# Two attentions in one kernel: normalisation in place in PSUM, eight score slots for VectorE, other staging buffers, hinted branches, and an order planned anew with five more VectorE tiles

## The chip, the core and the metric

The kernel runs on one core of a Trainium2 chip. The metric is the device time of one execution in microseconds (us). Before the change it is 740.9 us, the median of three runs (740.27 to 741.24). TensorE is called PE here (PEld is its weight load), VectorE DVE, ScalarE ACT, GpSimd POOL and SyncE SP.

## What is computed

Two attention blocks over different inputs of the same size (S = 2048 tokens, D = 640, H = 32 heads of 20), their outputs side by side:

```
def _A_ref(x, wqkv, wo):                      # softmax attention
    qkv = (x @ wqkv).reshape(B, S, 3, H, Dh) -> q, k, v per head
    p = softmax(einsum("bhqd,bhkd->bhqk", q, k) * Dh ** -0.5)
    return einsum("bhqk,bhkd->bhqd", p, v) -> (B, S, D) @ wo

def _B_ref(x, wqkv, wo):                      # linear attention
    phi = lambda t: where(t > 0, t + 1, exp(t)) + 1e-6
    num = phi(q) @ (phi(k)^T v);  den = phi(q) . sum_s phi(k) + 1e-6
    return (num / den) -> (B, S, D) @ wo

return concatenate([a, b], axis=-1)
```

A has 32 heads x 2048 x 2048 scores, and each needs an exponential. That is the bulk of the work.

## The kernel before, in words

**Head groups and score tiles.** The 32 heads are taken four at a time, the 2048 queries 512 at a time: 8 x 4 = 32 *head groups*, numbered n = 0 to 31 (`self.od`). Each has 16 key tiles of 128, and a key tile has four score units (one head each) of 128 x 512. A score unit is one matmul `f_Qr,f_KT` in a quarter of PE's rows; several of them, on different rows, run side by side.

**Two ways to an exponential.** Most key tiles go to ACT: two units at a time lie in a pair of PSUM banks (a *score group*; pairs 0, 1 and 2, 3 take turns), and one activation (L1880) writes 2 x 512 exps into two of the 16 slots of `f_PT`. With 146 tiles on the other way there are (512 - 146) x 4 / 2 = 732 such exps. The other 146 tiles, chosen by the list `DN` (how many of the five key tiles in `DKT` each head group gives away), go to DVE: it converts the scaled scores to int16 (L1778), so that the bits read as a bf16 are a rough power of two; POOL adds a constant into a second buffer (`int64_add`, L1964), a DMA with accumulate (issued by POOL at L1962, 512 KB) adds that buffer back on the first one, and POOL adds another constant (L1956). The first sum is used with V, the second with a scaled copy `f_Vp`, as two more PV terms. The buffers are `f_Sr`: `NS` = 4 slots for the first sum and `NY` = 3 for the second.

**PV and normalisation.** Per head group all PV matmuls (`f_PT,f_V`, `f_Sr,f_V`, `f_Sr,f_Vp`) add up in one PSUM bank, number 4 (`PVB`); groups go strictly one after the other. V's first column is one, so the bank holds the denominators too. `norm` (L1967 to L1992) ends a group on DVE: a 32 x 32 block transpose of the bank into `f_T` in SBUF, fp32 (L1991), after which the bank is free for the next group (`freed`); a reciprocal of the denominators (L1982); the multiply into `f_T2` (L1984); the transpose back into `f_OTn` (L1988). SP then copies the heads' rows into `f_OTd` by small DMAs (L2017), from which the output projection reads.

**The rest of PE's work** is the projections of A (`f_xT,f_wq`, `f_xT,f_ar`, `f_ar,f_xT` for Q, K and V), the output projections (`f_wo,f_OTd`, `f_wo,f_OTn`, and `f_ar` with 128 or 512 columns for B), all of B, and *fillers*, matmuls of zeros (`f_zt`) that keep PE's utilisation up. These *auxiliary* works and the DVE score tiles share the banks 5, 6 and 7. A wide matmul here has 512 columns; most come in fours (`quad`) that fill the four column tiles of the array side by side.

**The order.** Nothing is scheduled on the chip: while the program is built, `_Fast.run` plays the five engines against a clock of its own. Each pick takes the engine that is free first (`self.free`); `est` says when the operands and buffers of an operation are there; `try_pe` chooses among score group, PV, DVE tile, auxiliary step and filler, `try_q` the runnable operation of lowest `prio` on the other engines. `emit` and `burst` then write the instruction into that engine's stream and book a cost. So the costs in the class (`CDMA`, `LDMA` for the accumulating DMA, `SW` for a change of the matmul kind, the latency in `push`) and the goals (`B0`, `B1`, `DOUBLE`, `LASTD`, the `P` priorities) decide the order, and on the chip each engine walks through its list and waits, in order, for semaphores.

**Output staging.** `evac` copies a bank of a finished output projection into one of five 512-wide parts of `f_st` (L1009 on DVE, L1008 on ACT) and queues an output DMA on SP (L1006), with priority -1 (first) if the step's own priority is at most 0, else 55. x's first 512 rows land in `f_st` too, before it is used for that (`start_loads`).

**The end.** A flag is made on the chip from the reciprocals (it says whether all denominators are in range). All engines load it into a register (L2311), and `nc.If(val > 0)` (L2312, shown as L202 in the profile) runs a general version, `_general`, if it is set; on these inputs all engines branch over it, and SP waits for the last output DMAs.

## Time and profile before

| | |
|---|---|
| median of 3 runs | 740.9 us (740.27 to 741.24) |
| the profiled execution | 740.83 us; 739.1 us of it from the first to the last instruction (the span) |
| mean granted PE clock | 0.987 of full speed |
| ACT | 699.4 us busy, 732 exps at L1880 |
| DVE | 617.2 us busy |
| POOL | 455.1 us busy |
| PE | 711.8 us busy (ends modelled) |

How to read the lines in the prediction. A timeline row is start, length, engine, line, operation, out<-in, shapes, count, and in square brackets the idle time ahead of it with what ended it. A waits row is who waited <- for whom: sum, times, longest, in us. A row of a single line or tile gives shortest, median and longest duration in ns, then the first and last start. Buffer numbers are left out: `f_T` stands for `f_T` and `f_T2`, `ps` for any PSUM bank. A row in the window table has, behind its window and length, busy time and count of PE, PEld, DVE, ACT and POOL, then the granted PE clock, the DMA engines' busy share and GB/s. Engine names that end in q are the sequencer's own instructions (branches, semaphores, DMA issues).

### The profile page before, as it was taken

The page shows a single profiled execution, that of the slowest core. Times are in us where ns is not written, and L with a number is a line of the kernel's source. Part 1 is how long each engine was busy: PE and PEld are TensorE (multiplying, and loading weights), DVE is VectorE, ACT ScalarE, POOL GpSimd, SP SyncE. Part 2 cuts the span into 40 slices and gives each one's busy share as a digit, 9 for nine tenths or more (in the row PEclk, how much of TensorE's full clock was granted, in tenths as well). Part 3 has the DMA queues.
Part 4 walks back from the last instruction along what each step waited for, and adds up shares of the span by engine and source line. Part 5 has one row for each costly group of instructions (what it writes and reads, how often), then busy time and mean ns, then how long its engine had stood idle before and what let it go on. Part 6 is the DMA issues. An engine that isn't in the chain of part 4 may idle for free.

```text
span 739.1 us, 24693 instructions
## 1 busy us (share of the span) xinstructions
PE 711.8 (96%) x10762; PEld 247.1 (33%) x10762; DVE 617.2 (84%) x1087; ACT 699.4 (95%) x778; POOL 455.1 (62%) x469
## 2 busy tenths in 40 slices
...
GB/s 197 191 164 107 134 124 151 123 149 186 171 176 155 151 145 136 129 126 98 128 112 150 129 186 137 157 159 136 104 178 146 169 158 68 143 106 81 153 156 68
DMA packets 68107, 104.12 MB, mean 141 GB/s; under 512 B 33707, under 2 KB 48747, under 8 KB 67995
## 3 DMA queue, kind: packets, MB, share of 16 engines
...
q14 instruction: 28, 0.22, 0.1%
...
## 4 chain that ended last, share of the span: by engine, by line
ACT 63%; PE 18%; DMA 8%; DVE 6%; POOL 3%; issue 1%; SPq 1%; ACTq 0%; DVEq 0%
ACT f_PT L1880 61%; PE ps L166 18%; DMA f_Sr<-f_Sr 6%; DVE f_Sr L1778 3%; ACT f_ar L1415 2%; POOL f_KT L1147 1%; DMA f_OTd<-f_OTn 1%; POOL f_Sr L1964 1%; DVE f_ar L1417 1%; DMA f_ar<-in_A_wqkv_dram 1%; SPq L2017 1%; DVE f_T L1984 1%; DVE f_T L1991 0%; DVE f_OTn L1988 0%; POOL f_V L1131 0%
## 5 line engine op out<-in xcount | busy, mean ns | idle before, releaser
L1880 ACT ACTIVATE f_PT<-ps 128x1024 bf16<-128x1024 f32 x732 | 684.6, 1112 | 24.5 <-PE ps L166 23.7
L1778 DVE TENSOR_SCALAR f_Sr<-ps 128x512 int16<-128x512 f32 x584 | 390.4, 683 | 71.0 <-PE ps L166 65.6
L166 PE MATMUL ps<-f_Qr,f_KT 32*128 32x512 bf16 x2048 | 300.2, 387 | 8.9 <-ACT f_PT L1880 3.4
L1964 POOL INT64_ADD f_Sr<-f_Sr x146 | 154.0, 1055 | 170.7 <-DVE f_Sr L1778 153.5
L1956 POOL INT64_ADD f_Sr<-f_Sr x146 | 167.7, 1151 | 63.9 <-DMA f_Sr<-f_Sr 61.5
L166 PEld LDWEIGHTS ps<-f_Qr,f_KT 32*128 32x128 bf16 x2048 | 76.4, 91 | 255.5 <-ACT f_PT L1880 218.8
L166 PE MATMUL ps<-f_ar 128*32 128x512 bf16 (+6 forms) x3024 | 146.5, 297 | 0.9 <-DVE f_Sr L1778 0.6
L1962 POOL DMA_DIRECT2D f_Sr<-f_Sr x146 | 127.7, 875 | 30.4 <-POOL f_Sr L1964 28.8
L166 PE MATMUL ps<-f_PT,f_V 128*21 128x512 bf16 x1464 | 141.1, 386 | 0.2 <-DVE f_T L1991 0.2
L166 PEld LDWEIGHTS ps<-f_ar 128*32 128x32 bf16 x3024 | 56.5, 95 | 57.3 <-issue 36.8
L166 PE MATMUL ps<-f_Sr,f_V 128*21 128x512 bf16 x584 | 58.3, 384 | 4.6 <-DMA f_Sr<-f_Sr 3.9
L166 PE MATMUL ps<-f_Sr,f_Vp 128*21 128x512 bf16 x584 | 58.8, 388 | 0.3 <-POOL f_Sr L1956 0.2
L166 PEld LDWEIGHTS ps<-f_PT,f_V 128*21 128x21 bf16 x1464 | 35.6, 90 | 49.6 <-issue 41.8
L166 PE MATMUL ps<-f_zt 128*32 128x256 bf16 (+2 forms) x184 | 36.6, 291 | 1.6 <-DVE f_warm L1089 1.1
L166 PE MATMUL ps<-f_ar,f_xT 128*32 128x160 bf16 x1280 | 35.7, 234 | 0.3 <-DMA f_ar<-in_A_wqkv_dram 0.3
L166 PE MATMUL ps<-f_wo,f_OTd 128*32 128x512 bf16 (+3 forms) x608 | 30.6, 302 | 2.4 <-DMA f_OTd<-f_OTn 2.4
L1991 DVE STREAM_TRANSPOSE f_T<-ps 128x512 f32<-128x512 f32 x32 | 22.7, 708 | 12.1 <-PE ps L166 12.0
L166 PE MATMUL ps<-f_xT,f_ar 128*32 128x512 bf16 x400 | 31.7, 383 | 0.0
L1009 DVE CAST f_st<-ps 128x512 bf16<-128x512 f32 x38 | 25.8, 684 | 6.5 <-PE ps L166 6.3
L1417 DVE TENSOR_SCALAR f_ar<-f_ar 128x512 bf16<-128x512 bf16 x40 | 24.2, 606 | 8.4 <-ACT f_ar L1415 7.7
L1984 DVE TENSOR_TENSOR f_T<-f_T,f_Rt 128x512 bf16<-128x512 f32 x32 | 27.8, 869 | 0.3
L166 PEld LDWEIGHTS ps<-f_ar,f_xT 128*32 128x32 bf16 x1280 | 22.9, 96 | 15.3 <-issue 11.8
...
## 6 DMA issues: line engine op xcount, KB each, us to landing
f_Sr<-f_Sr POOLq DMA_DIRECT2D x146, 512.0 KB, 5.1
out_dram<-f_st SPq DMA_DIRECT2D x40, 128.0 KB
...
```

The costliest lines, as they stand in the source:

```text
L166: lambda e: e.matmul(out, lhsT, rhs, start=start, stop=stop, tile_position=tp, skip_group_check=sgc),
L1009: (lambda e: e.tensor_copy(sl, ps[:, b, 0:w])), (("ps", b),), (("stage", s),),
L1147: self.push("pool", lambda e, g=g: e.tensor_copy(self.KT[:, g, :], self.kb16[:, 1:2].broadcast_to([128, self.S])), ("kb16",), tuple(("K", ...
L1415: self.push("act", lambda e: e.activation(r1, src, AF.Exp), (("ps", b),), (rk,), _c_act(n), prio=0, ok=ok, after=lambda: self.push("dve", ...
L1417: "dve", lambda e: e.tensor_scalar(r1, r1, 1.0, 1e-6, op0=ALU.min, op1=ALU.add), (rk,), (rk,),
L1778: post = lambda: self.push("dve", lambda e: e.tensor_scalar(self.Sr[:, s, i, :], self.ps[:, b, :], 0.0, 32639.0 - self.PH[-1], op0=ALU.max ...
L1880: return _Op("act", lambda e: e.activation(self.PT[:, s0:s0 + n, :], ps[:, b0:b0 + n, :], AF.Exp, scale=math.log(2.0) / 128.0, bias=self.l ...
L1956: put(lambda e: e.int64_add(vy, vy, up2), (), ry, self.C64, self.C64 + 150, fin)
L1962: put(lambda e: e.dma_start(flat(a).bitcast(BF16), flat(y).bitcast(BF16), accum_op=ALU.add), ry, ra, self.CDMA, self.LDMA, third).dma = True
L1964: put(lambda e: e.int64_add(vy, va, up), ra, ry, self.C64, self.C64 + 150, add, lambda: d < self.NY or self.dphase[d - self.NY] == 2)
L1984: "dve", lambda e: e.tensor_tensor(T2v, Tv, R.unsqueeze(2).broadcast_to([128, 16, 32]), op=ALU.mult),
L1991: self.push("dve", lambda e: e.transpose(self.T[:], ps[:, b, :]), (("ps", b),), ("T",), 630, prio=-1, after=freed, ok=lambda: n == 0 or (" ...
```

## The change

Eight edits in one:

1. **Normalisation in place.** The first transpose writes back into bank 4; reciprocal and multiply read the bank; only after the multiply is the bank free. `f_T` (fp32, SBUF) is gone. All three operations now have priority -1.
2. **Slots.** `NS` is 5, so that `f_Sr` has 8 slots for 7.
3. **VectorE tiles.** `DN` sums to 151 for 146.
4. **Planner's costs and goals.** `LDMA` 6500 for 6000; each accumulating DMA starts, in the plan, no sooner than 2900 ns after the one before (`dfree`), with 2000 ns more in the first 32 us; SP's operations land 3200 ns after their issue for 2000; `DOUBLE`, `B1`, `P1`, `P3`, `LASTD`, `SW` have other values.
5. **Staging.** `f_st` has 3 parts of 512 for 5; the last five tiles of A's output are staged in exp buffers (`f_PT`, slot p), without the ring; only these have SP priority -1, all others 55.
6. **x's first rows** land in slots 8 to 12 of `f_PT`.
7. **Zeros.** `f_zt` is 128 wide and is read twice by a broadcast of stride 0; the ring for `f_OTn` has a name (`RING` = 3, as before); small tiles share one.
8. **Branch.** `nc.If` is written out as a compare-and-branch on each engine with two blocks, and each branch has a hint whose place is at the normalisation of head group 30 of 0 to 31.

```
     NPT = 16
-    NS = 4
+    NS = 5
     NY = 3
     CDMA = 880.0
...
-    LDMA = 6000.0
+    LDMA = 6500.0
...
-    DOUBLE = 0.0
+    DOUBLE = -8.0
...
-    DN = (4, 3, 4, 5, 5, 4, 5, 5, 5, 4, 5, 5, 4, 4, 5, 4, 5, 5, 5, 5, 5, 4, 5, 5, 5, 5, 3, 5, 4, 4, 5, 5)
+    DN = (4, 5, 4, 4, 5, 5, 4, 5, 5, 4, 5, 5, 5, 4, 5, 4, 5, 5, 5, 4, 5, 5, 4, 5, 5, 5, 5, 5, 5, 5, 5, 5)
...
-    LASTD = 8
+    LASTD = 4
...
-    SW = 112.0
+    SW = 107.0
...
+        if op.dma and e == "pool":
+            s = max(t + 1450.0, self.dfree)
+            self.dfree = s + 2900.0
+            op.lat += s - t - 1450.0 + (2000.0 if t < 32000.0 else 0.0)
...
-        x = {"dve": 150, "act": 180, "pool": 150, "sp": 2000}[eng]
+        x = {"dve": 150, "act": 180, "pool": 150, "sp": 3200}[eng]
...
-    def evac(self, b, o, w, eng, prio, dst, done):
+    def evac(self, b, o, w, eng, prio, dst, done, pt=None):
         ps = self.ps
-        s = self.slot(o)
-        sl = self.stage[:].rearrange("p t n -> p (t n)")[:, 512 * s:512 * s + w]
-        end = prio <= 0
+        if pt is None:
+            s = self.slot(o)
+            sl, res = self.stage[:, s, 0:w], ("stage", s)
+        else:
+            sl, res = self.PT[:, pt, 0:w], ("PT", pt)
+        end = pt is not None
...
+        if n == self.NN - 2:
+            self.hints = {e: self.nc.engines[e].mark_branch_hint_location() for e in mybir.ALL_ENGINES}
...
-        Tv = self.T[:].rearrange("p (b c) -> p b c", c=32)
+        Tv = ps[:, b, :].rearrange("p (b c) -> p b c", c=32)
...
-        self.push("dve", lambda e: e.transpose(self.T[:], ps[:, b, :]), (("ps", b),), ("T",), 630, prio=-1,
-                  after=freed, ok=lambda: n == 0 or ("OTn", n - 1) in self.done)
+            self.push("dve", lambda e: e.transpose(self.OTn[:, o, :], self.T2[:]), ("T2",), (("OTn", o),),
+                      630, prio=1, after=lambda: self.normed(n),
+                      ok=lambda: self.opv[n] is None or ("OTs", self.opv[n]) in self.done)
+        self.push("dve", lambda e: e.transpose(ps[:, b, :], ps[:, b, :]), (), (("ps", b),), 630, prio=-1,
+                  ok=lambda: n == 0 or ("OTn", n - 1) in self.done, after=lambda: self.push(
+                      "dve", lambda e: e.reciprocal(R, Tv[:, :, 0]), (("ps", b),), (("Rt", n),), 160, prio=-1,
                       after=lambda: self.push(
                           "dve", lambda e: e.tensor_tensor(T2v, Tv, R.unsqueeze(2).broadcast_to([128, 16, 32]),
                                                                op=ALU.mult),
...
+                          (("ps", b), ("Rt", n)), ("T2",), _c_dve(512), prio=-1, after=freed)))
...
-        with nc.If(val > 0):
+        for e in mybir.ALL_ENGINES:
+            nc.engines[e].br_lt(val, 1, on_true="f_last", on_false="f_general").branch_hint(kf.hints[e])
+        with nc.body("f_general"):
             sch.join()
             _general(nc, A_x, A_wqkv, A_wo, out)
+            nc.br("f_last")
+        nc.switch_bb("f_last")
         sch.finish()
```

Three places of PE's list follow, before and after (a row is line, operation, out<-in, size, and how many of the kind stand behind each other). `f_Qr,f_KT` are scores: a row of two or three is a score group, with one DVE score in it if three.

First, the PV of the first VectorE tile of head group 0 (`f_Sr,f_V`), near exp 14, before:

```order
L166 MATMUL ps<-f_Qr,f_KT 128x512 x3
L166 MATMUL ps<-f_Sr,f_V 21x512 x4
L166 MATMUL ps<-f_PT,f_V 21x512 x4
L166 MATMUL ps<-f_Qr,f_KT 128x512 x3
L166 MATMUL ps<-f_Sr,f_Vp 21x512 x4
```

and from the same score group on, after:

```order
L166 MATMUL ps<-f_Qr,f_KT 128x512 x3
L166 MATMUL ps<-f_PT,f_V 21x512 x4
L166 MATMUL ps<-f_ar,f_xT 32x160 x24
L166 MATMUL ps<-f_Qr,f_KT 128x512 x2
L166 MATMUL ps<-f_ar,f_xT 32x160 x16
L166 MATMUL ps<-f_Qr,f_KT 128x512 x3
L166 MATMUL ps<-f_PT,f_V 21x512 x4
L166 MATMUL ps<-f_ar,f_xT 32x160 x24
L166 MATMUL ps<-f_Qr,f_KT 128x512 x2
L166 MATMUL ps<-f_ar,f_xT 32x160 x16
L166 MATMUL ps<-f_Qr,f_KT 128x512 x3
L166 MATMUL ps<-f_Sr,f_V 21x512 x4
```

The tile's PV has moved behind four more score groups, and V projections have moved ahead of it.

Second, the boundary from head group 0 to 1, from score group 33 (the first row) to score group 34 (the last), before:

```order
L166 MATMUL ps<-f_Qr,f_KT 128x512 x2
L166 MATMUL ps<-f_xT,f_ar 32x512 x4
L166 MATMUL ps<-f_Sr,f_Vp 21x512 x4
L166 MATMUL ps<-f_xT,f_ar 32x512 x12
L166 MATMUL ps<-f_xT,f_wq 32x512 x8
L166 MATMUL ps<-f_PT,f_V 21x512 x8
L166 MATMUL ps<-f_xT,f_wq 32x512 x12
L166 MATMUL ps<-f_Sr,f_V 21x512 x4
L166 MATMUL ps<-f_PT,f_V 21x512 x4
L166 MATMUL ps<-f_Qr,f_KT 128x512 x2
```

and after, where ahead of these rows stand score group 33 (three matmuls), twelve `f_xT,f_ar` and four `f_Sr,f_V`; the rows of one or two scores but the last are DVE's, alone:

```order
L166 MATMUL ps<-f_Qr,f_KT 128x512 x2
L166 MATMUL ps<-f_xT,f_ar 32x512 x8
L166 MATMUL ps<-f_Sr,f_Vp 21x512 x4
L166 MATMUL ps<-f_Qr,f_KT 128x512
L166 MATMUL ps<-f_xT,f_wq 32x512 x20
L166 MATMUL ps<-f_xT,f_ar 32x512 x16
L166 MATMUL ps<-f_Qr,f_KT 128x512
L166 MATMUL ps<-f_xT,f_ar 32x512 x4
L166 MATMUL ps<-f_Sr,f_V 21x512 x4
L166 MATMUL ps<-f_PT,f_V 21x512 x12
L166 MATMUL ps<-f_ar,f_xT 32x160 x60
L166 MATMUL ps<-f_Qr,f_KT 128x512 x2
```

From 56 wide matmuls between the two groups it has gone to 88 wide and 60 of 160 columns.

Third, the end of PE's list, before the flag's matmul, before:

```order
L166 MATMUL ps<-f_wo,f_OTd 32x128 x16
L166 MATMUL ps<-f_wo,f_OTn 32x128 x4
L166 MATMUL ps<-f_wo,f_OTn 32x512 x16
L166 MATMUL ps<-f_wo,f_OTn 32x128 x16
L166 MATMUL ps<-f_gm,f_ones 1x2
```

and after (`f_sm` holds what `f_gm` and `f_ones` held; `f_ar` is B's last projection here):

```order
L166 MATMUL ps<-f_wo,f_OTn 32x128 x4
L166 MATMUL ps<-f_ar 32x128 x80
L166 MATMUL ps<-f_wo,f_OTd 32x512 x16
L166 MATMUL ps<-f_wo,f_OTn 32x512 x12
L166 MATMUL ps<-f_wo,f_OTn 32x128 x16
L166 MATMUL ps<-f_wo,f_OTd 32x512 x16
L166 MATMUL ps<-f_wo,f_OTn 32x512 x8
L166 MATMUL ps<-f_wo,f_OTd 32x512 x16
L166 MATMUL ps<-f_wo,f_OTn 32x512 x8
L166 MATMUL ps<-f_sm 1x2
```

B's last projection and three of the five output tiles of A's last query block (opening with `f_OTd`, closing with `f_OTn`) now stand at the very end.

More of the change, by code (lines that the diff above doesn't have):

```diff
@@ L803 @@
     B0 = 0.25
-    B1 = 0.88
-    P1 = 0
+    B1 = 0.96
+    P1 = -0.5
     P2 = -0.5
-    P3 = 2
+    P3 = 0
     P4 = 2
@@ L876, in __init__ @@
         self.bnext = 0.0
+        self.dfree = 0.0
         self.abank = list(self.AUX)
@@ L879, in __init__ @@
         self.chk = -1
-        self.stq = [[] for _ in range(5)]
+        self.stq = [[] for _ in range(self.NSTG)]
         self.log = []
@@ L893, in alloc @@
         self.wqp = self.sb("f_wqp", [128, _NP, N_DC, 128], BF16)
-        self.zt = self.sb("f_zt", [128, 256], BF16)
+        zt = self.sb("f_zt", [128, 128], BF16)
+        self.zt = zt[:]
+        self.zr = zt[:].unsqueeze(1).broadcast_to([128, 2, 128])
         self.wq = self.sb("f_wq", [128, N_DC, D_MODEL], BF16)
-        ar = self.sb("f_ar", [128, 20576], BF16)
+        ar = self.sb("f_ar", [128, 20480], BF16)
         self.ar = ar
@@ L924, in alloc @@
         self.PT = self.sb("f_PT", [128, self.NPT, 512], BF16)
+        self.xs = self.PT[:].rearrange("p t n -> p (t n)")[:, 4096:4096 + 4 * D_MODEL].rearrange("p (t n) -> p t n", t=4)
         self.Sr = self.sb("f_Sr", [128, self.NS + self.NY, 4, 512], I16)
-        self.T = self.sb("f_T", [128, 512], F32)
         self.T2 = self.sb("f_T2", [128, 512], BF16)
-        self.OTn = self.sb("f_OTn", [128, 3 + self.NX, 512], BF16)
+        self.OTn = self.sb("f_OTn", [128, self.RING + self.NX, 512], BF16)
         self.OTd = self.sb("f_OTd", [128, 5, 512], BF16)
         self.Rt = self.sb("f_Rt", [128, 16 * self.NN], F32)
-        self.stage = self.sb("f_st", [128, 4, D_MODEL], BF16)
+        self.stage = self.sb("f_st", [128, self.NSTG, 512], BF16)
         self.rd = self.sb("f_rd", [128, 2, 2, 24], F32)
         self.ident = self.sb("f_id", [128, 128], BF16)
-        self.kb = self.sb("f_kb", [128, 2], F32)
+        sm = self.sb("f_sm", [128, 8], F32)
+        self.kb, self.km, self.gm = (sm[:, 2 * k:2 * k + 2] for k in range(3))
+        self.warm, self.ones = sm[:, 6:7], sm[:, 7:8]
         self.kb16 = self.sb("f_kb16", [128, 2], BF16)
-        self.km = self.sb("f_km", [128, 2], F32)
-        self.gm = self.sb("f_gm", [128, 2], F32)
         self.g2 = self.sb("f_g2", [1, 2], F32)
         self.flag = self.sb("f_flag", [1, 1], I32)
-        self.warm = self.sb("f_warm", [128, 1], F32)
-        self.ones = self.sb("f_ones", [128, 1], F32)
         xf = self.xT[:].rearrange("p c s -> p (c s)")
```

48 lines of the change are left out of this document (23 added, 25 removed).

## The prediction

> **What bounds the kernel now.** I read the page first, for the shares of the engines, then ScalarE's (ACT's) timeline and its waits by stage, because the page says that ACT is the busiest with work that nothing else can replace. Two lines of the page, the first from its part 1, the second from its part 5:
>
> ```profile
> PE 711.8 (96%) x10762; PEld 247.1 (33%) x10762; DVE 617.2 (84%) x1087; ACT 699.4 (95%) x778; POOL 455.1 (62%) x469
> L1880 ACT ACTIVATE f_PT<-ps 128x1024 bf16<-128x1024 f32 x732 | 684.6, 1112 | 24.5 <-PE ps L166 23.7
> ```
>
> PE's 96% is of modelled ends; ACT's 95% is work. Of ACT's 24.5 us of pauses before exps, 23.7 end on a matmul (PE). Where they lie, ACT's timeline of the first 62 us shows (start, length of a run of exps, in brackets the pause ahead of it):
>
> ```profile
> 20.49 3.77 ACT L1880 ACTIVATE f_PT<-ps 128x1024 bf16<-128x1024 f32 x4 [2.86 <-PE ps L166]
> 26.07 2.85 ACT L1880 ACTIVATE f_PT<-ps 128x1024 bf16<-128x1024 f32 x3 [1.81 <-PE ps L166]
> 30.03 1.02 ACT L1880 ACTIVATE f_PT<-ps 128x1024 bf16<-128x1024 f32 x1 [1.10 <-PE ps L166]
> 32.75 1.02 ACT L1880 ACTIVATE f_PT<-ps 128x1024 bf16<-128x1024 f32 x1 [1.70 <-PE ps L166]
> 34.26 15.96 ACT L1880 ACTIVATE f_PT<-ps 128x1024 bf16<-128x1024 f32 x17 [0.48 <-PE ps L166]
> 52.72 10.19 ACT L1880 ACTIVATE f_PT<-ps 128x1024 bf16<-128x1024 f32 x11 [2.50 <-PE ps L166]
> ```
>
> and ACT's waits in 180 to 240, 360 to 500 and 500 to 715 us (sum, times, longest) show the rest:
>
> ```profile
> ACT f_PT L1880 <- PE ps L166: 2.1, 5, 0.8
> ACT f_PT L1880 <- PE ps L166: 6.5, 8, 1.7
> ACT f_PT L1880 <- PE ps L166: 0.5, 2, 0.3
> ```
>
> So ACT bounds the stretch from 53 to 727 us, with 9.1 us of pauses in it, and PE bounds the first 53 us. What makes the later pauses, the chain of waits tells (start, length, what), with PE's waits for DMAs (sum, times, longest) and four 10 us windows (the eighth figure behind the colon pairs, after POOL, is the granted PE clock):
>
> ```profile
> 23.09 7.99 DMA f_Sr<-f_Sr
> 172.94 7.62 DMA f_Sr<-f_Sr
> 425.00 7.69 DMA f_Sr<-f_Sr
> 572.66 33.17 ACT f_PT L1880 x36
> ```
>
> ```profile
> PE ps L166 <- DMA f_Sr<-f_Sr: 3.9, 5, 1.1
> PE ps L166 <- DMA f_OTd<-f_OTn: 2.4, 2, 1.8
> ```
>
> ```profile
> 26.00:36.00 10.00, 7.71 (x122) 2.39 (x118) 6.02 (x10) 6.51 (x7) 4.01 (x4) 0.83 0.61 157
> 176.00:186.00 10.00, 8.72 (x74) 2.59 (x73) 7.24 (x13) 8.27 (x10) 6.27 (x7) 0.83 1.02 198
> 428.00:438.00 10.00, 8.70 (x89) 2.08 (x89) 5.73 (x9) 7.85 (x9) 5.87 (x6) 0.83 0.86 194
> 473.00:483.00 10.00, 9.48 (x88) 2.38 (x86) 8.80 (x13) 8.36 (x9) 6.76 (x8) 0.83 0.78 140
> ```
>
> The accumulating DMA of a VectorE tile took 7.6 to 8.0 us three times, where the planner had counted 6.0; PE, in order, stood about 1 us at each, and in the same windows the granted clock fell to 0.83 on the mean. Full clock for 6.6 us and half for 3.4 gives that. ACT lost 1.6 to 3.5 us of each window. These are the pauses that longer planned DMA times can take away.
>
> **The change, part by part.** *151 tiles, not 146.* Five tiles more on VectorE (DVE) take 5 x 4 = 20 score units, 10 exps, from ACT. An exp costs its pitch, 33.17/36 = 0.921 us, not the 1.112 of the group, which overlaps: **-9.2 us** of ACT. DVE gets 20 conversions, POOL 10 additions and 5 DMA issues:
>
> ```profile
> L1778 DVE TENSOR_SCALAR f_Sr<-ps 128x512 int16<-128x512 f32 x584 | 390.4, 683 | 71.0 <-PE ps L166 65.6
> f_Sr<-f_Sr POOLq DMA_DIRECT2D x146, 512.0 KB, 5.1
> ```
>
> 20 x 0.683 = 13.7 us on DVE lie in its 122 us of idle time, POOL has 284 us free: counted at nothing. Were that cover gone, PE would wait for the conversions, up to 13.7.
>
> *Normalisation in place.* The transpose keeps its size (rows of single lines: shortest, median, longest of one in ns):
>
> ```profile
> L1991 DVE STREAM_TRANSPOSE f_T<-ps x32: 699/706/718, 51.4 to 728.3; 128x512 f32<-128x512 f32 x32
> L1984 DVE TENSOR_TENSOR f_T<-f_T,f_Rt x32: 629/691/2056, 53.0 to 729.3; 128x512 bf16<-128x512 f32 x32
> L1609 DVE TENSOR_TENSOR f_ar<-ps,f_rd x24: 453/644/659, 458.5 to 683.4; 128x480 bf16<-128x480 f32 x16, 128x320 bf16<-128x320 f32 x8
> ```
>
> No row has a transpose that writes PSUM; between 0.70 and the 0.87 (27.8 us over 32) of the multiply as it is now, I take 0.71, as it reads the same bank. The multiply from PSUM has a near row: L1609 never exceeds 0.659 where L1984 reaches 2.056, so 0.644 x 512/480 = 0.69. DVE gets 3 to 6 us freer, off the path. What it costs is the accumulator bank: it comes free after transpose, reciprocal and multiply, 0.9 us later, 32 times, and behind it stand the PV matmuls of the next head group, and behind those, ACT, once its 16 exp buffers are full. At most boundaries PE has other work and ACT 8 exps of buffer; where they run out, the new order shows it, next.
>
> *The order.* I counted what PE does from one score group's start to the next one's, with prices from its timeline. Before, around the pause at 52.72 (the first and last row are score groups; between them stand 56 matmuls of 512 columns), a run of 60 of 160 columns, and two fours right behind each other:
>
> ```profile
> 50.44 0.39 PE L166 MATMUL ps<-f_Qr,f_KT 32*128 32x512 bf16 x2
> 53.89 0.39 PE L166 MATMUL ps<-f_Qr,f_KT 32*128 32x512 bf16 x2
> 24.32 1.22 PE L166 MATMUL ps<-f_ar,f_xT 128*32 128x160 bf16 x60
> 46.04 0.40 PE L166 MATMUL ps<-f_Sr,f_V 128*21 128x512 bf16 x4
> 46.26 0.39 PE L166 MATMUL ps<-f_Sr,f_Vp 128*21 128x512 bf16 x4
> ```
>
> 58 wide matmuls took 53.89 - 50.44 = 3.45 us, 0.0595 each (0.22/4 = 0.055 where nothing but fours follow each other), and 3.45 less one exp pitch, 0.92, is 2.53: the pause. In the changed order 91 wide and 60 of 160 stand there: 5.4 + 1.2, and 0.3 to 0.6 more since four of the scores go alone, not in fours. That is some 7.0, a pause of 6.0, 3.5 more than before. It holds the wait for the PV of head group 0, whose VectorE tiles are due later now, and the late bank. One boundary on, from score group 55 to 56, stand 39 wide and 48 of 160 (2.3 + 1.0): a pause of 2.4 that was not there. At the boundary from head group 23 to 24, group 555 to 556, stand 35 wide and 80 of 128 (2.1 + 1.1 by the price of the tail's, below, and 0.2 for a lone score): 2.4 too. Sum **+8.3 us**; if a wide matmul goes at 0.055 there, 7.
>
> Against that, PE no longer stands at late DMAs. At exps 14 and 15 the first tile's PV moves behind four score groups, 3.7 us later, past the landing: 1.70 + 0.48 may go. The 9.1 us later on may go too: accumulates are now planned with 6.5 us and one behind another, SP's small copies with 3.2 for 2.0, which bears on the 2.4 us at OTd. Bounds: 0 and -11.3; new ones of 2 are possible, since 5 more DMAs share the queues. I take **-6.5**, somewhat over half: the three longest DMAs have a place each, the window at 473 us has none of them.
>
> [...]
>
> *The tail.* Rows of the timeline's last 15 us (PE, DVE):
>
> ```profile
> 725.99 0.39 PE L166 MATMUL ps<-f_Qr,f_KT 32*128 32x512 bf16 x2
> 729.42 0.40 PE L166 MATMUL ps<-f_wo,f_OTd 128*32 128x128 bf16 x16
> 729.70 0.40 PE L166 MATMUL ps<-f_wo,f_OTd 128*32 128x128 bf16 x16
> 730.80 1.27 PE L166 MATMUL ps<-f_wo,f_OTn 128*32 128x512 bf16 x32 [0.36 <-DVE f_OTn L1988]
> 731.33 1.89 DVE L1009 CAST f_st<-ps 128x512 bf16<-128x512 f32 x3 [0.27 <-PE ps L166]
> 733.87 0.14 DVE L2070 TENSOR_SCALAR f_flag<-f_g 1x1 int32<-1x1 f32 x1
> ```
>
> From the last score group to the flag it is 8.0 us. Behind that group stand 68 wide and 96 narrow matmuls before, 116 and 176 after: B's last projection and two of A's openings have moved there. 48 wide at 0.055 to 0.0595 are 2.6 to 2.9, 80 narrow at 0.28/20 (20 lie between the starts of the second and third row) are 1.1. Off go the 0.36 of waiting for the normalisation, which now lies under PE's work, and some 0.8 since one conversion, not three, lies between the last matmul and the flag: **+2.7** (2.5 to 2.8).
>
> *Branch hints.* Single lines again (ns, first and last start):
>
> ```profile
> L202 PEldq COMPARE_BRANCH  x1: 3879/3879/3879, 734.9 to 734.9; - x1
> L202 SPq EVENT_SEMAPHORE  x12: 27/28/28, 735.1 to 736.3; - x12
> L2303 POOLq DRAIN  x1: 2897/2897/2897, 735.3 to 735.3; - x1
> ```
>
> PE's branch over the general version takes 3.9 us, to 738.8, and the end waits for it. If a hint removes that, POOL's drain (735.3 + 2.9 = 738.2) is late next: **-0.6**; if the drain shrinks too, SP's waits, to 736.3, are late next: -2.5; if a hint does nothing, 0. [...]
>
> *Counted at nothing:* x staged in exp buffers 8 to 12 (they are read long before the first exp, whose scores are made from them), the repeated zero tile (same 256 columns), small tiles in one. Output staging with 3 buffers for 5 and a late place in SP's queue costs nothing while SP is ahead of the 38 conversions that use it; without that cover up to 2 us, in the range.
>
> Sum against the profiled execution (740.83 us; its span is 739.1; median 740.9): -9.2 + 8.3 - 6.5 + 2.7 - 0.6 = -5.3, so **735.5 us**.
>
> **The rivals.** *All goes well* (chance 0.20): every late-DMA pause goes (-11.3), PE runs its packed places at 0.055 (+7), the hint brings 2.5: -9.2 + 7 - 11.3 + 2.5 - 2.5 = -13.5, 727; with half of what it has over the forecast, 731. For it: the planner's longer times stand just where the trace was late. Against: three longer queues on the same DMA engines.
>
> *Nothing comes out* (0.16): the stands only move: the DMAs of 512 KB come late at other tiles, and a pause term of -1.5 with the rest as counted gives -0.3: 740.5. For it: ACT's relief of 9.2 and the packed places of 8.3 are of one size, so that the DMA term decides alone. ACT's pauses would go from 23.7 to 30 us.
>
> *Slower* (0.14): the accumulator bank. At 32 boundaries PV starts 0.9 us later. If ACT's exp buffers are full at ten more of them, as they are at the places where I counted 2.4, each costs 0.9, and if the DMA term shrinks to nothing too, -5.3 + 9 + 6.5 gives 751; with half of the places 747, with half of the DMA term left 743. It decides from the point where PV lags over 8 exps behind. Against: between the counted places the order holds no score group with over 1 us of PE work more than ACT's pitch.
>
> **How the numbers follow.** The forecast's own case (0.50) spans 732 to 739. Faster by over 0.2% (1.5 us, about what a measurement of this kernel tells from no change): 0.50 x 0.98 + 0.20 + 0.16 x 0.15 = 0.71. Within: 0.15; slower: 0.14. The range leaves out the better half of the first rival and the worse half of the last: 730 to 743.
>
> **What would show it.** Right: 722 exps; ACT's pauses before exps in one block of about 6 us at 50 to 60 us, 2 to 3 at the boundary to head group 24, and no waits of PE for f_Sr's DMA over 1 us; clock rows at 1.00 between 160 and 480 us; over 10 us from the last score group to the flag; PE's branch far under 3.9 us. Wrong: ACT pauses spread over many boundaries (the bank), halved clock at new places (the DMAs), or a PE branch as long as before.

## The result and the profile after

The changed kernel takes 750.4 us, the median of four runs (749.5 to 754.6); the kernel before took 740.6 beside it (738.9 to 741.2). The ratio is 1.0147, with a 95% interval of 1.0105 to 1.0189: 10 us slower, where 735.5 was forecast. Some executions fall into a slower state with a lower clock (one of the six of after_if, below: 763.7 us at a mean clock of 0.972, the others 749.2 to 751.6 at 0.980 to 0.985); the medians here and below count every execution, the ratios leave the slow ones out. The profiled execution took 749.5 us, 8.6 us of span more than before. Three lines of its page, the first from part 1, the others from part 5; the first two answer to the two of before:

```profile
PE 713.9 (95%) x10809; PEld 246.2 (33%) x10809; DVE 621.1 (83%) x1107; ACT 690.6 (92%) x768; POOL 467.8 (63%) x484
L1892 ACT ACTIVATE f_PT<-ps 128x1024 bf16<-128x1024 f32 x722 | 674.8, 1107 | 34.8 <-PE ps L166 29.5
L1427 ACT ACTIVATE f_ar<-ps 128x512 bf16<-128x512 f32 x40 | 27.3, 683 | 3.2 <-PE ps L166 3.2
```

The 10 exps are gone, and ACT is busy 8.8 us less. Yet its pauses grew from 24.5 us to 38.0 (34.8, and 3.2 ahead of B's exps, which had none). ACT's timeline (start, length, in brackets the pause ahead) shows where; the runs of five and three exps go on beyond the edge of the view, and so do other rows of timelines:

```profile
28.79 17.67 ACT L1892 ACTIVATE f_PT<-ps 128x1024 bf16<-128x1024 f32 x19 [0.32 <-PE ps L166]
52.97 20.27 ACT L1892 ACTIVATE f_PT<-ps 128x1024 bf16<-128x1024 f32 x22 [6.51 <-PE ps L166]
75.42 4.71 ACT L1892 ACTIVATE f_PT<-ps 128x1024 bf16<-128x1024 f32 x5 [2.18 <-PE ps L166]
...
157.46 2.86 ACT L1892 ACTIVATE f_PT<-ps 128x1024 bf16<-128x1024 f32 x3 [4.48 <-DMA f_KT<-f_ar]
160.71 2.10 ACT L1892 ACTIVATE f_PT<-ps 128x1024 bf16<-128x1024 f32 x2 [0.40 <-PE ps L166]
163.30 3.09 ACT L1892 ACTIVATE f_PT<-ps 128x1024 bf16<-128x1024 f32 x3 [0.48 <-PE ps L166]
...
454.33 0.60 ACT L1427 ACTIVATE f_ar<-ps 128x512 bf16<-128x512 f32 x1 [2.95 <-PE ps L166]
457.10 1.02 ACT L1892 ACTIVATE f_PT<-ps 128x1024 bf16<-128x1024 f32 x1 [0.91 <-PE ps L166]
...
567.27 1.94 ACT L1892 ACTIVATE f_PT<-ps 128x1024 bf16<-128x1024 f32 x2 [2.46 <-PE ps L166]
...
696.12 1.94 ACT L1892 ACTIVATE f_PT<-ps 128x1024 bf16<-128x1024 f32 x2 [0.71 <-PE ps L166]
698.71 1.02 ACT L1892 ACTIVATE f_PT<-ps 128x1024 bf16<-128x1024 f32 x1 [0.65 <-PE ps L166]
718.92 12.94 ACT L1892 ACTIVATE f_PT<-ps 128x1024 bf16<-128x1024 f32 x14 [0.82 <-PE ps L166]
```

The pauses of 6.51, 2.18 and 2.46 us are the three packed places of the forecast (6.0, 2.4, 2.4), and those that stood at exps 14 and 15 are gone. New are the groups at 157, 454 and 696 us. What lies behind the first two, PE's timeline shows, and the waits for DMAs (sum, times, longest):

```profile
153.53 0.61 PE L166 MATMUL ps<-f_xT,f_wq 128*32 128x512 bf16 x8
158.54 0.61 PE L166 MATMUL ps<-f_Qr,f_KT 32*128 32x512 bf16 x3 [4.39 <-ACT f_PT L1892]
...
453.88 0.40 PE L166 MATMUL ps<-f_ar 128*32 128x512 bf16 x4 [3.88 <-DMA f_ar<-in_B_wqkv_dram]
```

```profile
ACT f_PT L1892 <- DMA f_KT<-f_ar: 4.5, 1, 4.5
DVE f_Sr L1790 <- DMA f_KT<-f_ar: 4.2, 1, 4.2
PE ps L166 <- DMA f_ar<-in_B_wqkv_dram: 3.9, 1, 3.9
PE ps L166 <- DMA f_Sr<-f_Sr: 0.7, 2, 0.4
```

At 153 us ACT, DVE, POOL and SP all wait for the same thing: the step `begin` of B puts a barrier on all four until K's last copies (`f_KT<-f_ar`, from buffers that B will use again) have landed. At 450 us PE waits for a piece of B's second weights. Both waits are no accident of one execution: the traces of after_if and after_pehint below, with their lists in the same order, have them too (ACT 4.4 and 4.3 us, PE 4.5 and 3.8). Two rows of the chain of waits (start, length) tell how long these two transfers took, 5.5 and 6.4 us from their issue:

```profile
151.75 5.53 DMA f_KT<-f_ar
447.43 6.40 DMA f_ar<-in_B_wqkv_dram
```

PE's waits for the accumulating DMAs (`f_Sr<-f_Sr`) fell from 3.9 us to 0.7: that part of the forecast came true. The third place has no DMA behind it. Two windows (busy time and count of PE, PEld, DVE, ACT, POOL; the granted clock is 1.00, then 0.51):

```profile
690.00:693.00 3.00, 2.32 (x18) 0.65 (x18) 3.00 (x8) 3.00 (x4) 2.21 (x3) 1.00 0.81 153
693.00:700.00 7.00, 6.89 (x48) 1.54 (x46) 4.63 (x8) 5.37 (x6) 3.48 (x4) 0.51 0.45 89
```

PE was busy 77% for 3 us, in pieces with no pause over 0.3 us, and then had half its clock for nearly 7 us. The end of the program, as single lines:

```profile
730.09 0.39 PE L166 MATMUL ps<-f_Qr,f_KT 32*128 32x512 bf16 x2
740.17 0.14 DVE L2083 TENSOR_SCALAR f_flag<-f_g 1x1 int32<-1x1 f32 x1
```

```profile
L2327 POOLq COMPARE_BRANCH  x1: 63/63/63, 740.9 to 740.9; - x1
L2327 PEldq COMPARE_BRANCH  x1: 497/497/497, 740.9 to 740.9; - x1
```

```profile
L2316 POOLq DRAIN  x1: 3312/3312/3312, 744.2 to 744.2; - x1
L2316 SPq DRAIN  x1: 7/7/7, 745.4 to 745.4; - x1
```

L2327 is the branch, and the drain of L2316 is the next thing that an engine does; POOL's (744.2, 3.3 us long) ends last. From the last score group to the flag it is 10.2 us (over 10 was forecast, 8.0 before). PE's branch fell from 3.88 to 0.50 us. But POOL, which before went from branch to drain in 0.43 us, now needs 3.24, and its drain ends at 747.5: flag to end grew from 5.1 to 7.4.

### The profile page after: what moved, and what is told of

It is laid out like the page before. It is cut to its first block, busy times and chain, and to the rows that moved or that the text cites. A ratio compares the mean times of both kernels' runs of the same rounds, so it can differ in the third digit from the quotient of the medians.

```text
span 747.7 us, 24867 instructions
## 1 busy us (share of the span) xinstructions
PE 713.9 (95%) x10809; PEld 246.2 (33%) x10809; DVE 621.1 (83%) x1107; ACT 690.6 (92%) x768; POOL 467.8 (63%) x484
## 4 chain that ended last, share of the span: by engine, by line
ACT 50%; PE 36%; DVE 5%; DMA 5%; SPq 1%; issue 1%; POOL 1%; POOLq 0%; ACTq 0%
ACT f_PT L1892 48%; PE ps L166 36%; DVE f_Sr L1790 3%; ACT f_ar L1427 2%; DMA f_Sr<-f_Sr 2%; DMA f_ar<-in_A_wqkv_dram 1%; SPq L1224 1%; DMA f_ar<-in_B_wqkv_dram 1%; DMA f_KT<-f_ar 1%; DMA f_OTd<-f_OTn 0%; POOL f_Sr L1976 0%; PE ps L1039 0%; DVE ps L1999 0%; DVE f_sq L1248 0%; DVE f_ar L1264 0%
## 5 line engine op out<-in xcount | busy, mean ns | idle before, releaser
L1892 ACT ACTIVATE f_PT<-ps 128x1024 bf16<-128x1024 f32 x722 | 674.8, 1107 | 34.8 <-PE ps L166 29.5
L1790 DVE TENSOR_SCALAR f_Sr<-ps 128x512 int16<-128x512 f32 x604 | 404.9, 683 | 82.5 <-PE ps L166 73.3
L1976 POOL INT64_ADD f_Sr<-f_Sr x151 | 160.0, 1060 | 176.0 <-DVE f_Sr L1790 109.9
L1968 POOL INT64_ADD f_Sr<-f_Sr x151 | 176.1, 1171 | 45.0 <-DMA f_Sr<-f_Sr 43.6
L1974 POOL DMA_DIRECT2D f_Sr<-f_Sr x151 | 133.0, 893 | 30.1 <-POOL f_Sr L1976 26.4
L166 PE MATMUL ps<-f_PT,f_V 128*21 128x512 bf16 x1444 | 135.9, 386 | 0.7 <-issue 0.3
L166 PE MATMUL ps<-f_Sr,f_V 128*21 128x512 bf16 x604 | 60.2, 385 | 0.9 <-DMA f_Sr<-f_Sr 0.7
L166 PE MATMUL ps<-f_zt 128*32 128x256 bf16 (+2 forms) x211 | 42.5, 289 | 1.1 <-DVE f_sm L1100 1.1
L166 PE MATMUL ps<-f_ar,f_xT 128*32 128x160 bf16 x1280 | 33.6, 234 | 0.9 <-DMA f_ar<-in_A_wqkv_dram 0.8
L1427 ACT ACTIVATE f_ar<-ps 128x512 bf16<-128x512 f32 x40 | 27.3, 683 | 3.2 <-PE ps L166 3.2
L1999 DVE STREAM_TRANSPOSE ps<-ps 128x512 f32<-128x512 f32 x32 | 23.2, 725 | 6.4 <-PE ps L166 6.2
```

What stands on the lines that cost most here:

```text
L166: lambda e: e.matmul(out, lhsT, rhs, start=start, stop=stop, tile_position=tp, skip_group_check=sgc),
L1427: self.push("act", lambda e: e.activation(r1, src, AF.Exp), (("ps", b),), (rk,), _c_act(n), prio=0, ok=ok, after=lambda: self.push("dve", ...
L1790: post = lambda: self.push("dve", lambda e: e.tensor_scalar(self.Sr[:, s, i, :], self.ps[:, b, :], 0.0, 32639.0 - self.PH[-1], op0=ALU.max ...
L1892: return _Op("act", lambda e: e.activation(self.PT[:, s0:s0 + n, :], ps[:, b0:b0 + n, :], AF.Exp, scale=math.log(2.0) / 128.0, bias=self.l ...
L1968: put(lambda e: e.int64_add(vy, vy, up2), (), ry, self.C64, self.C64 + 150, fin)
L1974: put(lambda e: e.dma_start(flat(a).bitcast(BF16), flat(y).bitcast(BF16), accum_op=ALU.add), ry, ra, self.CDMA, self.LDMA, third).dma = True
```

## The experiments

Each experiment was timed beside the kernel before, so its ratio goes to that; medians from different experiments lie up to 3 us apart for the kernel before itself (737.8 to 741.0). In the first four, *after_if* has the branch as before; every list is otherwise in the same order.

```
-        for e in mybir.ALL_ENGINES:
-            nc.engines[e].br_lt(val, 1, on_true="f_last", on_false="f_general").branch_hint(kf.hints[e])
...
+        with nc.If(val > 0):
```

> The changed kernel with the branch made as in the kernel before (nc.If, no hints); every engine's list is otherwise the same. Theory (the hints cost POOL more than they save PE): PE's branch takes 3.9 us again, POOL goes from its branch to its drain in 0.4 us for 3.3, and the span ends with PE or with SP's last waits (745.4 in the changed kernel): 1.9 to 2.3 us shorter, 748.3. Rival (POOL's 3.3 us are due to where its code lies or to the output DMAs still under way, not to the hint): the gap stays and the time is 750.4, or 750.4 and PE late as well, no shorter.

*After_pehint*: a hint for PE alone, the two blocks written out.

```
-            nc.engines[e].br_lt(val, 1, on_true="f_last", on_false="f_general").branch_hint(kf.hints[e])
+            br = nc.engines[e].br_lt(val, 1, on_true="f_last", on_false="f_general")
+            if e in kf.hints:
+                br.branch_hint(kf.hints[e])
```

> The changed kernel with a hint for PE's branch alone; the branch is still written out as two blocks. Theory (a hint speeds up PE's branch and slows POOL's): PE's branch 0.5 us, POOL's gap between branch and drain 0.4 us, the end is set by SP's last waits or POOL's drain: 2.0 us shorter, 748.4. Rival (the two written-out blocks make POOL's gap, whatever the hint): POOL's gap stays 3.3 us, time 750.4.

*Before_hint*: edit 8 alone in the kernel before, that is, the cut shown for after_if the other way round, with the hints' place in `norm`.

> The kernel before with edit 8 alone (written-out branch, a hint on each engine). The prediction's term: PE's branch 0.5 us for 3.9, 0.6 us shorter (740.0), up to 2.5 if POOL's drain shrinks too. Theory now: POOL's gap from branch to drain grows from 0.4 to 3.3 us, its drain ends at 741.5 instead of 738.2, the span is 2.5 us longer: 743.1.

*After_kqsp*: one line of the barrier is moved.

```
             sch.barrier(("dve", "act", "pool", "sp"),
-                        (... + tuple(("kq", k, x) for k in range(2) for x in range(NQC)) + ...))
+                        (... + ...))
+            sch.barrier(("sp",), tuple(("kq", k, x) for k in range(2) for x in range(NQC)))
```

> The changed kernel, where at the start of B only SP waits for the last K copies (their buffers are written next by SP's loads alone); ACT, DVE and POOL wait there for the other buffers only. No list is in another order. Theory (a wait for DMAs at 153 to 157 us stops ACT, then PE, and the clock halves): ACT's 4.5 us wait on f_KT goes, and the 1.1 us of pauses under the halved clock with it: 5.6 us shorter, 744.8. Rival 1 (only the wait goes, PE loses the clock there anyway): 4.5 shorter, 745.9. Rival 2 (ACT's pause is made up later, since PE bounds the boundaries behind it): under 1.5 shorter, 749 to 750.

After_if took 751.3 us (ratio to before 1.0172, 1.0134 to 1.021), after_pehint 752.9 (1.0191, 1.0155 to 1.0228), before_hint 739.95 against 738.8 (1.0021, 0.9986 to 1.0056). My theory on hints fell: POOL's gap is 2.83 us without any hint, 3.53 with one on PE alone, and 0.43 in before_hint with one on each engine. In before_hint PE's branch took 0.50, and flag to end 4.9 us for 5.1: DVE, 3.75 us from its branch to its drain, came last. So the hint shortens PE's branch and is worth 0.1 to 0.2 us by these two traces; the times can't tell it from nothing.

After_kqsp took 748.8 us (1.0151, 1.0109 to 1.0194): 1.6 less than the median of the changed kernel, by the ratio no less at all (1.0147), and in any case not 5.6. Rival 2 (under 1.5 shorter) is nearest. ACT's timeline shows that the wait is wholly gone, and what stands in its place 38 us later; below them PE's row there:

```profile
138.22 27.71 ACT L1893 ACTIVATE f_PT<-ps 128x1024 bf16<-128x1024 f32 x30
...
195.69 0.60 ACT L1427 ACTIVATE f_ar<-ps 128x512 bf16<-128x512 f32 x1 [2.25 <-PE ps L166]
197.73 1.02 ACT L1893 ACTIVATE f_PT<-ps 128x1024 bf16<-128x1024 f32 x1 [0.48 <-PE ps L166]
199.59 4.69 ACT L1893 ACTIVATE f_PT<-ps 128x1024 bf16<-128x1024 f32 x5 [0.83 <-PE ps L166]
```

```profile
195.02 0.62 PE L166 MATMUL ps<-f_ar 128*32 128x512 bf16 x4 [2.48 <-DMA f_ar<-in_B_x_dram]
```

5.4 us of pauses went, 3.6 came. SP still waits for K's copies, and B's loads of x stand behind that in its queue. In the changed kernel PE has no wait for x there; its stall had held it back long enough for them to arrive.

*After_kq_wb* also plans the second weight load with about its measured time (6.0 us). Beside it ran single edits and the change without edit 4; each of them gives a new order too:

```
     def load_wB(self, part, src, key, lat=3500):
...
-            self.load_wB(0, self.Bw[:, 0:D_MODEL], ("wl", 0, 1))
-            self.load_wB(1, self.Bwo, ("wl", 1, 1))
+            self.load_wB(0, self.Bw[:, 0:D_MODEL], ("wl", 0, 1), lat=6000)
+            self.load_wB(1, self.Bwo, ("wl", 1, 1), lat=6000)
```

> The changed kernel with two mends: at the start of B only SP waits for the last K copies, and the planner counts 6.0 us, not 3.5, for the second load of B's weights (in the trace of the changed kernel its last piece took 6.4 us from issue to PE's matmul). The order is the same up to about 440 us and another one behind it. Theory (the two waits for DMAs, 4.5 us at 157 and 3.9 at 454, cost ACT their length and 1 to 2 us more each under the halved clock): ACT's pauses from 442 to 471 us go, 10 to 12 us in all, and 1.5 to 2.5 at the boundary to head group 24, where less is packed now: 737 to 740. Rival (the stands only move to other DMAs or packed places of the new order behind 440 us): pauses of 4 us and more at other exps from 442 on, 744 to 749.

*Before_151*: the changed kernel's list in the kernel before.

```
-    DN = (4, 3, 4, 5, 5, 4, 5, 5, 5, 4, 5, 5, 4, 4, 5, 4, 5, 5, 5, 5, 5, 4, 5, 5, 5, 5, 3, 5, 4, 4, 5, 5)
+    DN = (4, 5, 4, 4, 5, 5, 4, 5, 5, 4, 5, 5, 5, 4, 5, 4, 5, 5, 5, 4, 5, 5, 4, 5, 5, 5, 5, 5, 5, 5, 5, 5)
```

> The kernel before with edit 3 alone: 151 tiles by the new list, in four slots, with the old costs and goals; its order is another one. The prediction's term: ACT has 10 exps of 0.921 us less, -9.2. By the theory that new packed places give part of it back, one of 2 to 4 us stands at the boundary to score group 148 and nothing as large elsewhere, late DMAs as before: 733 to 736. Rival (each tile given to VectorE makes as many new stands as it saves, since PE has 20 PV matmuls and 5 more DMAs to wait for): 738 to 744.

*Before_inplace*: the changed `norm`, without the hints' place, in the kernel before.

```
-        Tv = self.T[:].rearrange("p (b c) -> p b c", c=32)
+        Tv = ps[:, b, :].rearrange("p (b c) -> p b c", c=32)
...
-        self.push("dve", lambda e: e.transpose(self.T[:], ps[:, b, :]), (("ps", b),), ("T",), 630, prio=-1,
-                  after=freed, ok=lambda: n == 0 or ("OTn", n - 1) in self.done)
+        self.push("dve", lambda e: e.transpose(ps[:, b, :], ps[:, b, :]), (), (("ps", b),), 630, prio=-1,
```

> The kernel before with edit 1 alone: transpose in place in bank 4, reciprocal and multiply from it. The prediction's rival: bank 4 is held 0.9 us longer at 32 boundaries and ACT loses 0.9 at ten or more of them, spread over the kernel: 746 to 750. Theory: the hold costs nothing at most boundaries, since PE has other work there; what it costs is by the order, which moves 28 wide and other matmuls into the place before score group 34, 2 us more there, and 2 in smaller ones: 741 to 745.

*After_oldcosts*: edit 4 undone (`DOUBLE`, `B1`, `P1`, `P3`, `LASTD` and `SW` likewise).

```
-    LDMA = 6500.0
+    LDMA = 6000.0
...
-            s = max(t + 1450.0, self.dfree)
-            self.dfree = s + 2900.0
-            op.lat += s - t - 1450.0 + (2000.0 if t < 32000.0 else 0.0)
...
-        x = {"dve": 150, "act": 180, "pool": 150, "sp": 3200}[eng]
+        x = {"dve": 150, "act": 180, "pool": 150, "sp": 2000}[eng]
```

> The changed kernel with edit 4 undone (LDMA 6000, no spacing of the accumulating DMAs, 2000 for SP, the old goals). Theory (edit 4's order put the last K copies right before the start of B and the second load of B's weights right before its use): no wait of ACT for f_KT near 157 us and none of PE for f_ar's weights near 454; late accumulating DMAs are back, PE's waits for f_Sr's DMA 3 to 6 us for 0.7, the place before score group 34 has 60 wide matmuls and a pause of 4 for 6.6: 743 to 748. Rival (these waits come with 151 tiles and eight slots, whatever the costs): both waits are there, 750.

| kernel | us, median | ratio to before, 95% |
|---|---|---|
| after_kq_wb | 745.3 | 1.0074 (1.0039 to 1.011) |
| before_151 | 767.6 | 1.0387 (1.0335 to 1.044) |
| before_inplace | 761.7 | 1.026 (1.0204 to 1.0316) |
| after_oldcosts | 771.4 | 1.0432 (1.0379 to 1.0486) |

After_kq_wb's time lies in its rival's range (744 to 749), but without the rival's pauses of 4 us: PE's wait for the weights fell from 3.9 to 1.5 us, ACT's 2.95 at 454 to 0.58, and no exp behind 442 us has a pause of 1 us. Against the changed kernel some 5 us are gained (1.0074 for 1.0147), where the theory asked 10 and more. The other three were far outside what either theory gave. Their waits for DMAs, of before_inplace first, of before_151 second, and third of before_null2, a kernel without any of the eight edits that comes below:

```profile
PE ps L166 <- DMA f_Sr<-f_Sr: 7.0, 5, 2.3
ACT f_PT L1880 <- DMA f_KT<-f_ar: 5.6, 1, 5.6
```

```profile
PE ps L166 <- DMA f_Sr<-f_Sr: 3.5, 5, 1.1
ACT f_PT L1880 <- DMA f_KT<-f_ar: 5.3, 1, 5.3
```

```profile
DVE f_Sr L1778 <- DMA f_KT<-f_ar: 2.3, 1, 2.3
ACT f_PT L1880 <- DMA f_KT<-f_ar: 1.6, 1, 1.6
```

The wait for K's copies is there with either edit and with none, and DVE waits 4.2 us for them in after_oldcosts: it belongs to the order and to no edit. In before_151 it is the smaller part of the loss. Its last exp ends at 733.2 us, 5.4 later than in the kernel before (727.8), but 31.3 us follow to the end of the span, for 11.3: a part of B was left over for PE and DVE behind the last exp. The bank, the mechanism of the prediction's "slower", is not it: PE and its weight loads wait 1.4 us in all for the multiply that frees bank 4 in the changed kernel (L2003), and 2.1 for the transpose that freed it before (L1991); in before_inplace, with edit 1 alone, the weight loads wait 1.1 us for the multiply (L1989):

```profile
PEld ps L166 <- DVE f_T L2003: 1.2, 4, 0.4
PE ps L166 <- DVE f_T L2003: 0.2, 1, 0.2
```

Next, POOL's gap and two attempts at a faster kernel. *Before_pool62* and *after_kq_wb_pool* add instructions to POOL's list that wait for what has long happened:

```
     def norm(self, n):
         qc, g = self.od[n]
+        pool = self.sch.eng["pool"]
+        for _ in range(112 * (n + 1) // self.NN - 112 * n // self.NN):
+            pool.h.wait_ge(self.sch.sems[pool.sem], 1)
```

(112 of them become 62 instructions; the second kernel has 356 in that place, which become 191.)

> The kernel before with 62 more instructions in POOL's list, spread over the 32 normalisations: waits on POOL's own semaphore for a value it has long reached, so POOL's branch stands at place 576 as in the changed kernel (572), not 514. Theory (POOL's gap between branch and drain depends on where branch and target lie in its code, not on hints or on the new order): the gap grows from 0.43 to about 3 us with this alone, and the drain ends 2.6 us later against the flag, behind PE's branch: flag to end 6.9 to 7.5 us for 5.0. Rival (the gap belongs to something else in the changed kernel, such as SP's output DMAs still under way): the gap stays 0.43 and flag to end 5.0.

> The kernel with the two mends and 191 more such instructions in POOL's list, so that its branch stands at place 754 for 563. [...]

In both the gap went with the place of POOL's branch. Before_pool62 as single lines, branch and drain:

```profile
L202 POOLq COMPARE_BRANCH  x1: 53/53/53, 735.5 to 735.5; - x1
```

```profile
L2306 POOLq DRAIN  x1: 2925/2925/2925, 739.4 to 739.4; - x1
```

The gap is 3.86 us with the branch at place 576 (0.43 at 514 in the kernel before), and flag to end 7.9 (6.9 to 7.5 was expected); the only execution took 744.3 us against 741.0. In after_kq_wb_pool, at place 754, the gap is 0.42, flag to end 5.2 us instead of 7.2 without the added instructions, and the time 744.6 (1.0034, 1.0 to 1.0067).

*Replan_a* and *replan_b*, both with the two mends and POOL's added instructions:

```
replan_a:  B1 = 0.92   DOUBLE = -4.0   SW = 105.0   DLEAD = 22
replan_b:  DLEAD = 22   DN[22], DN[23] = 5, 4   (for 4, 5)
```

> An attempt at a faster kernel: the last one with other planner goals (B1 0.92, DOUBLE -4, SW 105, DLEAD 22), 151 tiles, both mends, POOL's branch at place 747. Counted by matmuls between score groups, as in the prediction, its packed places hold 1.6 us more pauses than the mended order's, and 4.7 us less work stands behind its last score group. Theory (packed places and the tail decide): about 3 us under the kernel with the mended POOL gap, 741. Rival (a new order has stands at DMAs of its own that no count of matmuls shows, as the kernel before with 151 tiles had): 745 to 755, with PE or ACT waits on DMAs of 2 us and more at new places.

> A second attempt: the mended kernel with one VectorE tile moved from head group 23 to 22 and DLEAD 22, POOL's branch at place 746. By the count its packed places hold 0.9 us less pauses than the mended order's, and as much stands behind the last score group. Theory (packed places decide): 743. Rival (new stands at DMAs): 747 to 755.

Replan_a took 748.5 us (1.0088, 1.005 to 1.0125): its rival was right, with a wait of 2.8 us for B's x and 1.2 for accumulating DMAs. Replan_b took 741.2 (1.0002, 0.9964 to 1.0041), 2 less than its theory said, level with the kernel before and 9 us under the changed kernel. No order was found that beats the kernel before.

Last, with four executions each, the question what an edit is worth and what a new order: a number of the planner is moved that means nothing on the chip.

```
before_null1:  SW = 111.0    (112.0)        after_null1:  SW = 106.0    (107.0)
before_null2:  STEP = 19.0   (20.0)         after_null2:  STEP = 19.0   (20.0)
```

> The kernel before with SW 111 for 112: no instruction is another, only their order. Theory (the order of the kernel before is an uncommonly good draw; any new draw from the old costs has late accumulating DMAs and stands at the start of B): 755 to 768, as with the single edits. Rival (the single edits themselves cost 20 us and more): 738 to 745.

> The kernel before with STEP 19 for 20, the time that the planner lets pass when an engine has nothing to do; again only the order is new. Theory: 755 to 768. Rival: 738 to 745.

> The changed kernel with SW 106 for 107; only the order is new. Theory (with edit 4's longer DMA times a new draw is about as good as the changed kernel's): 747 to 757, packed places by the count 6 us more than the changed kernel's. If the changed kernel's order is itself an uncommonly good one of its kind: 760 and more. If it is a bad one: 735 to 745.

> The changed kernel with STEP 19 for 20; only the order is new. Theory: 745 to 755, packed places by the count 3 us more. Uncommonly good order of the changed kernel: 760 and more. Bad one: 735 to 743.

Before_null1 took 783.2 us against 737.8 (1.0597, 1.0499 to 1.0695), before_null2 766.4 (1.0381, 1.0292 to 1.0469), after_null1 767.5 (1.04, 1.0337 to 1.0463), after_null2 755.6 (1.0247, 1.0177 to 1.0317). Before_null2 came as its theory said, after_null2 0.6 us above it; before_null1 was 15 us worse than its theory's 768, and after_null1 fell under the case "an uncommonly good order" of the changed kernel. Of before_null1, ACT's exps and two waits for DMAs:

```profile
L1880 ACT ACTIVATE f_PT<-ps 128x1024 bf16<-128x1024 f32 x732 | 687.6, 1102 | 60.6 <-PE ps L166 55.3 <-DMA f_Qr<-f_sq 3.8
```

```profile
PE ps L166 <- DMA f_Sr<-f_Sr: 11.9, 11, 2.4
ACT f_PT L1880 <- DMA f_Qr<-f_sq: 3.8, 1, 3.8
```

But for 23 more fillers (207 for 184), no instruction is another than in the kernel before, and yet 45 us: 36 us more of ACT's pauses, PE's waits for accumulating DMAs three times as long, a wait at the start of B. The clock goes with it: its mean over the profiled execution is 0.958 for 0.987, which is 33 us of clock lost ((1 - clock) x span) for 10. On the kernel before, an order drawn anew costs 29 and 45 us, the two edits tried there with a new order (1 and 3) 21 and 27: no more than the order alone. Among the orders tried here the kernel before has the best; of the changed kernel's kind, the two null orders are worse than its own, and those of after_kq_wb and replan_b, with the mends, better.

## Why the prediction was wrong

Point by point, on the spans of the two profiled executions (-5.3 forecast, +8.6 measured):

- **10 exps fewer, -9.2.** Right: there are 722 exps, and ACT's busy time fell by 8.8.
- **Packed places, +8.3.** Right in mechanism and nearly in size: 6.51 (6.0), 2.18 (2.4), and 2.46 at the third (2.4) with 1.3 more behind it. Against the 2.50 of before that is +10.0. Counting matmuls between two score groups works.
- **Late DMAs, -6.5.** This is the step that failed. Before, pauses outside the start and the packed places summed to 12.0 us (24.5 less 4.2 ahead of the first exp, 5.8 at exps 6, 10 and 13, and 2.5). After, the same sum is 16.2 (38.0 less 4.3, 5.0 and 12.5): +4.2, so the term is off by 10.7 us. The half that the prediction named happened, PE's stands at accumulating DMAs all but vanished. But the bounds, "0 and -11.3; new ones of 2 are possible", priced only the stands that the trace of before showed. A new order has its own: 5.4 us at the barrier of B, 5.0 at its weights (from 454 to 471 us), 1.8 from 696 to 700 us under half a clock. The rival "the stands only move" had the mechanism and looked at the wrong DMAs, those of 512 KB; the ones that came late were small copies and weight loads of SP, for which the planner counts 3.9 and 3.5 us from the issue and which took 5.5 and 6.4.
- **Tail, +2.7.** Measured 10.2 - 8.0 = +2.2.
- **Hint, -0.6.** PE's branch became short, as said. But the step overlooked DVE, whose drain ended at 738.8 in the kernel before, 0.1 us ahead of PE's, so that even there hardly 0.1 us was to be had, as before_hint shows. And it took POOL's own end as fixed, which came 7.2 us after the flag for 4.2, and the end of the program 2.3 later (+2.3), not by the hint: POOL's branch stands at place 572 of its list for 514. That the place sets the gap is shown, by 62 added instructions in one kernel (0.43 to 3.86 us) and 191 in another (to 0.42): in the 18 kernels the gap was 0.42 to 0.43 us with POOL's branch at places 511 to 528 and 746 to 754, and 2.8 to 4.2 at 563 to 576. Why the place does it, no run shows.
- **Counted at nothing.** The hold of bank 4, the staging and the zeros did cost nothing that the waits show.

The five measured terms (-8.8, +10.0, +4.2, +2.2, +2.3) add up to +9.9 for 8.6; the first exps, in no term, paused 0.7 less (9.3 us for 10.0), and 0.6 has no place. Of the signs that the prediction named for being wrong, "halved clock at new places" is the one that came: at 157, 454 and 693 us.

Behind the value of the late-DMA term stood what the trace of before showed: the clock fell in windows where PE stood about 1 us at late DMAs. In the runs, half clock came behind stands of PE of 4.39 us at 157 (0.50 from 158 to 164 us) and 3.88 at 454 (0.57 from 454 to 458), behind one of 2.48 at 195 in after_kqsp (0.81 over 190 to 198 us), and at 693, where PE was 77% busy with no pause over 0.3 us (0.51). In the four windows of the kernel before that the prediction shows it came too (0.83 on the mean, 0.50 in single microseconds such as 32 to 33 and 435 to 436), with no stand of PE over 1.2 us in them. What sets the clock, no run shows. The reading of the trace stands; the value did not follow from it.

Behind all terms lies one error of method: the sum set an edited order against one particular good order as if only the named places differed. The null runs show how much of the result is that. Of kernels with the old DMA times and a new order, five took 762, 766, 768, 771 and 783 us; of those with edit 4's, the changed kernel and its two null runs took 750, 756 and 768, and with the mends after_kq_wb, replan_a and replan_b 745, 749 and 741. That speaks for edit 4, its DMA times and goals together, which also shows in PE's waits for accumulating DMAs: 3.5 to 11.9 us in the first five, none to 3.5 in the others. That the edits as such make a better kernel than the old ones, order apart, is not shown; orders would have to be drawn many times on both sides.

## What to carry to other kernels

Where an edit feeds a planner, a scheduler or any rule that sets the order, first move one of its numbers by nothing and time that: here null changes cost 5 and 17 us on the changed kernel (755.6 and 767.5 against 750.4; 7 and 19 by the ratios) and 29 and 45 on the kernel before, where the edits were to bring 5. A good order is a part of the kernel. Price a new order by what it puts close together, every DMA with its reader and every barrier with the last transfer it waits for, not by the stands that the old trace shows. And a stall that is taken away can hand its time to the next transfer of the same queue: 5.4 us at B's barrier came back as 3.6 at B's input.

## What the runs showed of the chip

- **The time goes with the granted clock.** The same program took 732.5 us at a mean clock of 0.996 and 742.6 at 0.985: 10.1 us more for 8.2 us of clock lost ((1 - clock) x time), beside the first experiments. Over all 17 executions there it is about 1 us of time for 1 us of clock lost, with a scatter of some us: at 0.992 they took 736.3 to 742.1. Which of the two causes the other, these numbers don't say. So the 0.2% that the prediction named as the measurement's limit was too fine; the intervals above are some 0.35% to either side with six to twelve executions, and 0.7 to 1.0% with four.
- **Half clock came without an idle PE**: 77% of (modelled) busy time over 3 us, with no pause over 0.3 us, stood ahead of it at 693 us in the changed kernel (0.50 from 694 to 698 us). In two runs with the same list it came near there too: after_if had 0.55 from 694 to 698 us behind 77% of busy time from 690 to 693, after_kqsp 0.50 behind 78%.
- **A branch hint helped PE alone, and not always**: PE's branch took 0.41 to 0.50 us in nine of eleven kernels with a hint and 3.47 and 3.83 in replan_a and after_oldcosts, 3.56 to 4.25 without one; ACT and DVE took 2.7 to 4.0 us from branch to drain with and without.
- **POOL's last drain** took 2.89 to 2.93 us with 146 accumulating DMAs (the kernel before, before_null1, before_null2, before_pool62) and 3.31 to 3.32 with 151 (the changed kernel, after_null1, after_null2, after_kq_wb_pool); why, no run shows.
